# Hand-listed step order of a chunk-selecting attention and feed-forward kernel: where GpSimd issues its first loads, one copy moved to ScalarE, fewer warm-up matmuls, and two transposes moved ahead of two loads

## The chip, the cores and the metric

One Trainium2 chip, of which the program uses one core. The metric is device time in microseconds (us) of one execution; lower is better. A core has TensorE (PE: matrix products into the accumulator memory PSUM), VectorE (DVE), ScalarE (ACT), GpSimd (POOL) and SyncE (SP, which here only issues transfers). Each engine runs its own instructions in order; engines wait for each other through semaphores. Transfers (DMA) between the chip's main memory and on-chip memory are issued by SP and ACT (hardware queues, q1 and q10 in the profile) and by POOL (software queue, q0, which also converts float32 to bfloat16), and all of them are carried by the same 16 DMA engines.

## What is computed

```python
B, H, S, D = 4, 8, 768, 64;  chunk = 32;  top_k = 6
k_min, k_max = min and max of k over each chunk of 32 keys
ub = sum_d max(q * k_min, q * k_max)            # a bound for each query and chunk
top_chunks = the 6 chunks with the largest ub, among those not in the future
scores = q @ k.T / sqrt(D), masked to those chunks and to earlier positions
attn_out = softmax(scores) @ v
x = attn_out, heads side by side                 # 3072 tokens x 512
xn = x / rms(x) * rms_g
out = (silu(xn @ w_gate) * (xn @ w_val)) @ w_out # 512 -> 1536 -> 512
```

Inputs and output are float32; the products are in bfloat16, the bound `ub` in float32.

## The kernel before

The 3072 tokens are cut into 12 blocks of 256, listed in `ORDER` (L340). A block is written (b, m): batch b, third m of its sequence. The first five are (0,0), (1,0), (2,0), (3,0), (0,1); "block 0" to "block 11" count along this list. Heads are taken in two groups g = 0, 1 of four. An operation on (b, m, g) carries these numbers in its name.

What a block does in attention, with the engine and line:

- `load k…` and `load q…` (L431) fetch k and q in float32 into the tiles `kraw` and `qraw`. For blocks 0, 1 and 2 ("packed", L351) k is four transfers of 128 KB and q four more; later blocks take eight of 64 KB each. They are issued by SP, and for blocks 0 and 1 by SP and ACT in turn. `HELD` (L429) makes the first k load and the first q load of block 2 wait until the weight piece wg1 has landed, and those of block 3 until wo0 has landed.
- `load v…` (L456) fetches v in two transfers of 128 KB, e = 0 and 1, issued by POOL. `load v001` is e = 1 of block (0,0).
- `turn k`, `turn q` (DVE, L636) transpose `kraw` and `qraw` into `kT` and `qT`; `half k`, `half q` (L643 on ACT, L644 on POOL) copy them to bfloat16 (`kb`, `qb`).
- `ext0`, `ext1` (DVE, L651) take the minimum and maximum of a chunk, `dk` (POOL, L657) their difference; `bd0`, `bd1` (L676) place them in `BO`; `relu` (L731, L733) makes max(q, 0).
- `upper` (PE, L540, or L522 for m > 0) forms `ub`; `ubn`, `bar`, `top`, `mk`, `mt` (DVE, L565 to L591) choose the chunks and `swap` (L597, L601) crosses the mask to the other half of the partitions.
- `scores` (PE, L760, mask added in L771), `exp` (ACT, L810), `tri` (POOL, L780: causal triangle). For blocks 0 and 1 the scores of a block come in two parts: `a` (first 128 queries, needs no mask) and `b`.
- `values` (PE, L836), then `rden` and `norm` (DVE, L851, L855) divide and write `xnat`. `values(0,0,1)0` is group 1, first 128 tokens of block (0,0).

Then `square` (ACT, L872), `rms` (POOL, L878), `scale` (L906 on ACT, L890 on DVE). Blocks 0 to 3 go through `turn(i, …)` (PE transposes, L916) and `xsT` (L929); blocks 4 and later through `across` (L896), a transposing DMA that SP issues, two for each block (`across40` and `across41` for block 4). Blocks with m > 0 need a crossed copy of q: `qx` (L692) and, from block 4 on, four small transfers `qm0` to `qm3` on SP (L706), after which `relu` and `upper` can run.

The feed-forward (`ffn`, L937) is `wg` and `wv` (PE, L960), `tanh` (ACT, L967), `tg` (DVE, L971), `vcopy` (ACT, L979) with `hh` (POOL, L982) or `hh` on DVE (L975), then `project` (PE, L1008) and `out`. A name such as `wg(0,(0,)).4` is block 0, first 128 tokens, hidden tiles from 4 on. The weights come in thirds: wg0, wg1, wg2, wv0, wv1, wv2 (L464) and wo0 to wo2 (L469), 512 KB each in bfloat16, all issued by POOL. Hidden tiles 0 to 3 need the third 0, 4 to 7 the third 1, 8 to 11 the third 2.

Nothing decides the order at run time. `Plan.STEPS` (L47) lists all operations in one order, written as numbers: x // 8 is the operation, x % 8 its engine (0 PE, 1 ACT, 2 DVE, 3 POOL, 4 SP); each engine gets its own operations in that order. `Plan.SLOTS` (L156) gives the buffer that each operation takes. A negative number in `STEPS` is a run of warm-up matmuls (`keep_busy`, L1072) on the identity matrix, whose results nobody reads: -592 is 37 × 16 + 0, which is 18 matmuls of 512 columns into buffer F0; an even factor means 128 columns.

```python
n, slot = divmod(-x, 16)
fill[-1](n // 2, slot, n % 2)
```

Of the kernel before, what the change touches and what calls it, by code (L numbers as in the profile page):

```python
# [33 lines left out]
class Plan:  # L34
# [13 lines left out]
        27, 228, 233, 249, 244, 131, 123, 34, 155, 3, 99, 257, 276, 291, 281, 268, 299, 83, 412,  # L48
        425, 203, 67, 107, 75, 433, 420, 538, 115, 139, 315, 466, 323, 473, 482, 380, 396, 443, 490,
        545, 42, 498, 404, 307, 522, 388, 529, 506, 594, 515, 179, 611, 562, -592, -544, -320, 616,  # L50
        601, 554, 672, 626, 681, 571, 50, 457, 578, 786, 587, 634, 689, -82, -82, 792, 642, 57, 650,
        699, 848, 802, 9, 810, 857, 818, 658, 865, 826, 834, 665, 1098, 875, 841, -144, 704, 451,
        -80, 736, 912, 713, 746, 922, 754, 1107, 721, 930, 1185, -82, -114, 880, 961, 19, 1042, 731,
        889, 1114, 971, -82, 760, 897, 1058, 1049, 907, 1066, 331, 1130, 977, 1660, -211, -195,
        1248, 936, 1628, 1075, 1257, 1082, 1170, 1091, 1644, 195, -48, -128, 1192, 1684, 1177, 1362,
        1138, 1676, 1202, 1668, 1147, 1265, 1210, -48, 984, 770, 1154, 1163, 1636, 778, 1123, 946,
        1652, -49, 1368, 954, 1218, 1001, 1275, 994, 1424, 1433, 1226, -51, 1312, 1378, 8384, 1011,
        1234, 1441, 1322, 1242, 1386, 8344, 1330, 147, 1451, 1017, 1394, 1402, 339, 1280, 1410,
        8369, 1418, 1024, 1289, 1488, 347, 8336, 1498, 1297, 1034, 355, 8401, 1506, 1456, 8353,
        8480, 1307, 8410, 1537, 363, 8362, 1336, 8497, 8488, 1547, 1346, 1762, 1473, 8528, 8506,  # L60
        1465, 1851, 8513, 1354, 1483, 8536, 1778, 8545, 8379, 1553, 1706, -51, 1512, 8392, 8561,
        1522, 1530, 371, 1834, 1560, 1577, 8432, 8523, 1570, 8417, 8554, 8696, 8449, 1587, 1722,
        8688, 8458, 8721, 8571, 1593, 1730, 8584, 8705, 1802, 1739, 171, 2001, 1600, 1747, 8714,
# [1043 lines left out]
```

## Time and profile before

| what | us |
|---|---|
| three executions, median (lowest to highest) | 289.77 (289.53 to 289.91) |
| the profiled execution, whole | 291.3 |
| its span, first to last instruction | 289.5 |
| PE busy in the span | 278.6 |
| DVE busy | 215.8 |
| ACT busy | 207.0 |
| POOL busy | 167.8 |

The granted TensorE clock was 1.000 over the whole span. PE is busy for 96% of it, with 83 of its matmuls being warm-ups. The transfers move 31.94 MB, at a mean of 110 GB/s, but not evenly: the DMA engines are occupied without a break from about 2 us to 43 us, while block 0 and 1 and all weights are loaded.

How to read the rows below: in a timeline a row is start, duration, engine, line, operation, output<-input, shapes, count, and in brackets how long the engine had been idle and what the profile takes for the end of the wait. "SPq", "POOLq" or "DMA_DIRECT2D" mark the issuing of a transfer, not the transfer. The bracket names the event that came last by the profile; where the engine named had long been done, a transfer is often the true cause.

### The profile page before, as it was taken

To read this page: it belongs to the slowest core of one execution; us is meant where nothing else is said; L and a number is where in the kernel's file an instruction comes from. 1 tells how busy PE (TensorE), PEld (TensorE's weight loads), DVE (VectorE), ACT (ScalarE), POOL (GpSimd) and SP (SyncE) were. 2 spreads that over 40 slices of the span, in tenths; PEclk is the share of its full clock that TensorE was granted. 3 is DMA by queue.
4 is the path that set the end of the run, shared out by engine and by line. 5 is a ranking of instruction groups with operands and counts; after the bars stand their busy time and mean duration, and the time that the engine had idled before them with its cause. 6 is when DMAs were issued, how large, how long until landed. Compare 5 with 4: busy or idle time off the path is not lost.

```text
span 289.5 us, 11368 instructions
## 1 busy us (share of the span) xinstructions
PE 278.6 (96%) x4675; PEld 211.6 (73%) x4703; DVE 215.8 (75%) x626; ACT 207.0 (72%) x355; POOL 167.8 (58%) x268
## 2 busy tenths in 40 slices
PE   8989999999999998999999999999999999999995
PEld 2657897758877856888776786688678866588763
DVE  3978888888989999699989999987573724374341
ACT  2977887778979987867966695877679767564421
POOL 9668789979969874557693485527225206112420
PEclk9999999999999999999999999999999999999999
DMA  9999999897499494469699814913012200312023
GB/s 171 204 199 239 206 212 131 130 181 119 104 168 144 116 201 91 95 101 166 106 173 164 152 28 96 123 8 75 2 28 85 22 3 2 109 20 58 0 72 111
DMA packets 86388, 31.94 MB, mean 110 GB/s; under 512 B 74816, under 2 KB 81728, under 8 KB 86336
## 3 DMA queue, kind: packets, MB, share of 16 engines
q1 hardware_dynamic: 55616, 22.56, 33.7%
q0 software_dynamic: 29712, 7.87, 27.3%
q10 hardware_dynamic: 1008, 0.79, 1.4%
q8 instruction: 37, 0.61, 0.9%
q14 instruction: 15, 0.12, 0.1%
HBM read 28.58 MB, written 6.29 MB: 120 GB/s over the span
## 4 chain that ended last, share of the span: by engine, by line
PE 89%; DVE 3%; issue 2%; ACT 2%; SPq 1%; POOL 1%; DMA 1%; DVEq 0%; POOLq 0%
PE F L960 42%; PE F L1008 21%; PE S L760 8%; PE F L836 7%; PE F L1075 4%; PE S L771 3%; PE F L522 3%; SPq L376 1%; PE F L540 1%; ACT pt L810 1%; DVE kx L651 1%; DMA qraw<-in_q_dram 1%; PE F L916 1%; DVE kT L636 0%; DVE tg L971 0%
## 5 line engine op out<-in xcount | busy, mean ns | idle before, releaser
L810 ACT ACTIVATE pt<-S 128x1024 bf16<-128x1024 f32 (+3 forms) x104 | 85.5, 857 | 29.1 <-PE S L771 25.7
L982 POOL TENSOR_TENSOR hh<-tg,vs 128x512 bf16<-128x512 bf16 x48 | 55.1, 1157 | 43.5 <-DVE tg L971 27.8
L960 PE MATMUL F<-xsT,wg 128*128 128x256 bf16 (+1 forms) x640 | 72.2, 262 | 1.1 <-ACT pt L810 1.1
L960 PE MATMUL F<-xsT,wv 128*128 128x256 bf16 (+1 forms) x640 | 71.7, 262 | 0.1
L1008 PE MATMUL F<-wo,hh 128*128 128x512 bf16 (+1 forms) x272 | 65.6, 370 | 1.8 <-issue 0.6
L971 DVE SCALAR_TENSOR_TENSOR tg<-th,F 128x512 bf16<-128x512 bf16 x72 | 48.4, 679 | 23.9 <-ACT th L967 18.6
L960 PEld LDWEIGHTS <-wg 128*128 128x128 bf16 x640 | 55.8, 98 | 9.8 <-issue 1.5
L960 PEld LDWEIGHTS <-wv 128*128 128x128 bf16 x640 | 56.1, 98 | 7.8 <-issue 0.2
L967 ACT ACTIVATE th<-F 128x512 bf16<-128x512 f32 x72 | 42.5, 599 | 12.7 <-PE F L960 11.4
L780 POOL TENSOR_SCALAR_AFFINE_SELECT pt<-pt 128x512 bf16<-128x512 bf16 x48 | 31.9, 670 | 27.6 <-ACT pt L810 27.5
L1008 PEld LDWEIGHTS <-hh 128*128 128x128 bf16 x300 | 27.6, 98 | 25.2 <-issue 0.4
L979 ACT ACTIVATE vs<-F 128x512 bf16<-128x512 f32 x48 | 28.5, 598 | 9.8 <-PE F L960 6.6
L760 PE MATMUL S<-qb,kb 32*128 32x256 bf16 (+1 forms) x800 | 32.7, 253 | 0.9 <-ACT kb L643 0.7
L651 DVE TENSOR_REDUCE kx<-kT 128x16 f32<-128x512 f32 x48 | 31.1, 670 | 0.2
L836 PEld LDWEIGHTS <-pt 128*128 128x128 bf16 x672 | 25.5, 98 | 5.1 <-issue 1.2
L836 PE MATMUL F<-VX,pt 128*128 128x65 bf16 x672 | 27.6, 194 | 1.1 <-issue 0.7
L975 DVE TENSOR_TENSOR hh<-tg,F 128x512 bf16<-128x512 bf16 x24 | 16.1, 682 | 10.3 <-PE F L960 10.0
L760 PEld LDWEIGHTS <-kb 32*128 32x128 bf16 x800 | 13.5, 92 | 13.5 <-issue 11.6
L376 POOL DMA_DIRECT2D VX<-in_v_dram x24 | 22.9, 955 | 0.0
L636 DVE STREAM_TRANSPOSE kT<-kraw 128x512 f32<-128x512 f32 x24 | 16.4, 693 | 6.3 <-DMA kraw<-in_k_dram 4.1
L771 PE MATMUL S<-mtd,chunkrow 32*128 32x128 bf16 (+2 forms) x384 | 20.3, 203 | 0.0
L855 DVE TENSOR_TENSOR xnat<-F,rden 128x256 bf16<-128x256 f32 x48 | 19.5, 415 | 0.7
(73 smaller groups left out, 338.8 us busy)
## 6 DMA issues: line engine op xcount, KB each, us to landing
out_dram<-osb SPq DMA_DIRECT2D x23, 256.0 KB, 2.5
kraw<-in_k_dram SPq DMA_DIRECT2D x72, 64.0 KB, 3.3
qraw<-in_q_dram SPq DMA_DIRECT2D x72, 64.0 KB, 3.2
VX<-in_v_dram POOLq DMA_DIRECT2D x24, 128.0 KB, 4.8
QX<-qT SPq DMA_DIRECT2D x32, 64.0 KB, 3.0
wv<-in_moe_w_val_dram POOLq DMA_DIRECT2D x3, 512.0 KB, 11.2
wg<-in_moe_w_gate_dram POOLq DMA_DIRECT2D x3, 512.0 KB, 13.4
wo<-in_moe_w_out_dram POOLq DMA_DIRECT2D x3, 512.0 KB, 10.4
```

The source lines that it names most:

```text
L651: plan.op(f"ext{n}{J}", "DVE", 0.585, 0.67, lambda n=n, op=op: VE.tensor_reduce(out=at(kx)[:, g, n], in_=at(kT).rearrange("p h (j c x) -> ...
L760: TE.matmul(s[a // 2][:, a % 2, c0:c0 + q1 - q0], kbt[r, t, ks], qbt[r, t, q0:q1], start=(t == 0), stop=(t == 1 and not mask), skip_group_ ...
L771: TE.matmul(o, chunkrow[r, BLK * kg + P * e:BLK * kg + P * (e + 1)], mv, start=False, stop=(d == 1), skip_group_check=True)
L780: GE.affine_select(out=d, in_=d, compare_op=ALU.is_ge, fill=0.0, base=0, pattern=[[0, 4], [1, P]], channel_multiplier=-1)
L810: lambda pt=pt, hs=hs, c0=c0, c1=c1, x=sc[hp]: SE.activation(out=at(pt)[:, hs, c0:c1], in_=at(x)[:, :, c0:c1], func=ACT.Exp, scale=SCALE), ...
L836: TE.matmul(o[:, a, :], p_[:, a, off:off + P], vt[:, e, 4 * g + a, :], start=(kb_ == 0 and a == 0), stop=(kb_ == nkb - 1 and a == 3), skip ...
L960: TE.matmul(at(p_)[:, n * W:(n + 1) * W], w[:, g, ht * P:(ht + 1) * P], at(xT)[:, g, x0:x0 + W], start=(g == 0), stop=(g == NP - 1), skip_ ...
L967: plan.op(f"tanh{U}.{hp}", "ACT", 0.48, 0.6, lambda th=th, gp=gp: SE.activation(out=at(th), in_=at(gp), func=ACT.Tanh, scale=0.5), pri - 0 ...
L971: VE.scalar_tensor_tensor(out=at(tg), in0=at(th), scalar=1.0, in1=at(gp), op0=ALU.add, op1=ALU.mult), pri - 30, reads=[th, gp], writes=[tg ...
L979: plan.op(f"vcopy{U}.{hp}", "ACT", 0.48, 0.6, lambda vs=vs, vp=vp: SE.activation(out=at(vs), in_=at(vp), func=ACT.Copy), pri + 0.1, reads= ...
L982: plan.op(f"hh{U}.{hp}", "POOL", 1.11, 1.16, lambda tg=tg, vs=vs, hh=hh: GE.tensor_tensor(out=at(hh), in0=at(tg), in1=at(vs), op=ALU.mult) ...
L1008: TE.matmul(at(op)[:, cs], at(key)[:, o:o + P], wo[:, ht, cs], start=(ht == 0), stop=(ht == NHT - 1), skip_group_check=True)
```

## The change

Only `STEPS` and `SLOTS` differ. In the text of the diff nearly the whole start of `STEPS` changes:

```diff
-        27, 228, 233, 249, 244, 131, 123, 34, 155, 3, 99, 257, 276, 291, 281, 268, 299, 83, 412,
-        425, 203, 67, 107, 75, 433, 420, 538, 115, 139, 315, 466, 323, 473, 482, 380, 396, 443, 490,
-        545, 42, 498, 404, 307, 522, 388, 529, 506, 594, 515, 179, 611, 562, -592, -544, -320, 616,
...
+        27, 228, 233, 249, 244, 131, 123, 34, 155, 3, 99, 257, 276, 83, 203, 281, 67, 268, 107, 291,
+        75, 115, 412, 425, 299, 433, 420, 538, 139, 466, 380, 396, 473, 482, 490, 404, 545, 42, 498,
+        388, 522, 506, 515, 179, 594, 529, 611, 315, -288, -656, 616, 562, 601, 672, 554, 626, 571,
...
```

Written out by engine, with the names of the operations, it is this. POOL, from its sixth operation on:

```diff
 eps, BO00,
-load v000, load v001, BD02, ones9, BD00, BO01, BD01, BO02, ones1,
-wv0, wg1, load v100, wg0,
-bd1(0,0,0), ones6, relu(0,0,0), dk(0,0,1), bd1(0,0,1), tri(0,0,0)a, tri(0,0,1)a,
-load v101, half q(1,0,0), half, tri(0,0,0)b, rms(0,(0,)), tri(0,0,1)b, wv1,
-dk(1,0,0), bd1(1,0,0), ones8, dk(1,0,1), bd1(1,0,1), half k(1,0,1), tri(1,0,0)a, rms(0,(1,)),
+BD02, ones9, BD00, BO01, load v000, BD01, BO02, load v001, ones1,
+bd1(0,0,0), ones6, relu(0,0,0), wv0, dk(0,0,1), bd1(0,0,1), wg1, tri(0,0,0)a, load v100,
+tri(0,0,1)a, half q(1,0,0), wg0, half, tri(0,0,0)b, rms(0,(0,)), dk(1,0,0), bd1(1,0,0),
+tri(0,0,1)b, load v101, ones8, dk(1,0,1), bd1(1,0,1), tri(1,0,0)a, wv1, rms(0,(1,)),
 ones2, tri(1,0,1)a, wg2, wv2, wo0, tri(1,0,0)b, wo1,
...
```

ACT, DVE and SP:

```diff
 ACT: half q(1,0,1), exp(1,0,0)0a1,
+half k(1,0,1),
 square01, exp(1,0,1)0a0,
...
 DVE: bd0(1,0,0), turn q(1,0,1),
-relu(1,0,1), ext1(1,0,1), ubn(1,0,0), bar(1,0,0), rden(0,0,0)1, bd0(1,0,1), norm(0,0,0)1,
+ext1(1,0,1), rden(0,0,0)1, norm(0,0,0)1, ubn(1,0,0), relu(1,0,1), bar(1,0,0), bd0(1,0,1),
 rden(0,0,1)1, norm(0,0,1)1, top(1,0,0), xsT(0,(0,)),
...
 SP: load k1210, store2.1,
+across40, across41,
 load q1210, load q1220,
-across40, across41,
 load q1201, qm0(2,1),
...
```

PE, up to the last warm-up (W18 is 18 warm-ups of 512 columns, w17 is 17 of 128 columns):

```diff
-W18, w17, w10, upper(0,0,0), scores(0,0,0)0a, W2, W2, upper(0,0,1), scores(0,0,1)0a, W4,
-scores(0,0,0)0b, W2, values(0,0,0)0, values(0,0,1)0, W2, W3, scores(0,0,1)0b, W2, values(0,0,0)1,
-W6, w6, scores(1,0,0)0a, values(0,0,1)1, W1, w4, upper(1,0,0), W1, turn(0,(0,)), W1, upper(1,0,1),
-scores(1,0,1)0a, W1, values(1,0,0)0,
+w9, W20, upper(0,0,0), scores(0,0,0)0a, W5, upper(0,0,1), scores(0,0,1)0a, W6,
+scores(0,0,0)0b, W1, values(0,0,0)0, values(0,0,1)0, W4, scores(0,0,1)0b, W4, values(0,0,0)1,
+W4, scores(1,0,0)0a, upper(1,0,0), values(0,0,1)1, W2, turn(0,(0,)), W1, upper(1,0,1),
+scores(1,0,1)0a, values(1,0,0)0,
 wg(0,(0,)).4, wv(0,(0,)).0, scores(1,0,0)0b, turn(0,(1,)), values(1,0,1)0, wg(0,(0,)).0,
 scores(1,0,1)0b, wg(0,(1,)).0, values(1,0,0)1, wv(0,(1,)).0, wg(0,(1,)).4, wv(0,(1,)).4,
-W1,
 values(1,0,1)1,
...
```

That is 46 wide and 37 narrow warm-ups before, 47 wide and 9 narrow ones after. From there on every engine has the same operations in the same order as before, but for SP's two transposes; in `SLOTS` about 160 PE operations along the whole kernel take another of the four PSUM buffers F0 to F3.

272 rows, old and new, of tables (SLOTS, STEPS) are left out of this document.

## The prediction

> **What bounds the kernel now.** First the busy times by stage. The columns after a stretch are its length, the busy times of PE, PE's weight loads, DVE, ACT and POOL, then the clock, the DMA share and GB/s.
>
> ```profile
> 45.00:100.00 55.00, 54.45 (x902) 41.12 (x911) 49.12 (x157) 45.94 (x85) 47.46 (x72) 1.00 0.87 141
> ```
>
> From 45 us on PE is busy for 54.45 of 55 us, and its order there does not change. Time can go only in the start and in the few holes later. The start looks as full, but warm-ups fill it, so PE's share says nothing there. The chain of waits (start, length, what) shows what the start hangs on:
>
> ```profile
> 17.43 1.30 DVE kT L636 x2
> ...
> 24.72 1.79 PE F L960 x32
> ```
>
> The first feed-forward products stand at its end, DVE's `turn k` of block (1,0) near its head. The timeline of DVE, and of PE in its last row:
>
> ```profile
> 14.87 0.74 DVE L855 TENSOR_TENSOR xnat<-F,rden 128x256 bf16<-128x256 f32 x2
> 17.43 1.30 DVE L636 STREAM_TRANSPOSE kT<-kraw 128x512 f32<-128x512 f32 x2 [1.82 <-ACT pt L810]
> 20.51 0.70 DVE L636 STREAM_TRANSPOSE qT<-qraw 128x512 f32<-128x512 f32 x1
> 23.63 0.67 DVE L929 TENSOR_TENSOR xsT<-F,rmsg 128x512 bf16<-128x512 bf16 x1
> 24.56 1.05 PE L960 MATMUL F<-xsT,wg 128*128 128x128 bf16 x16
> ```
>
> DVE stands idle for 1.82 us before `turn k`. The row names ACT's `pt`, which `turn k` does not read; it reads `kraw`. The four k loads of block (1,0), first and last issue and landing times:
>
> ```profile
> L376 SPq DMA_DIRECT2D kraw<-in_k_dram x4: 311/368/511, 6.4 to 8.2; - x4
> DMA to landing us min/median/max: 7.4/8.3/9.1
> ```
>
> The last, issued at 8.2, lands 9.1 later, at 17.3, and DVE starts at 17.43. So this landing, and not DVE's or PE's work, sets the time of the first feed-forward product. What shares the DMA engines with it was issued by POOL, and the rates by stage show at what cost:
>
> ```profile
> 1.97 1.99 POOL L376 DMA_DIRECT2D VX<-in_v_dram  x2
> 5.32 0.77 POOL L376 DMA_DIRECT2D wv<-in_moe_w_val_dram  x1
> 6.00:12.00 6.00, 6.00 (x111) 3.86 (x109) 5.85 (x19) 5.95 (x8) 4.23 (x10) 1.00 1.59 165
> 12.00:15.50 3.50, 3.48 (x68) 1.77 (x60) 2.77 (x14) 3.20 (x11) 2.53 (x4) 1.00 1.18 259
> 29.50:40.00 10.50, 9.85 (x186) 9.42 (x186) 9.41 (x18) 8.81 (x19) 7.85 (x16) 1.00 1.24 206
> ```
>
> While v is moving, all queues together reach 165 GB/s; with weights beside k and q 259; weights alone 206, so that a third of 512 KB takes 2.5 us.
>
> **Part by part: the loads.** Four memsets now stand before `load v000` and two more before `load v001`: v starts 0.8 to 1.3 us later. wv0 moves behind `relu(0,0,0)`, from 5.3 to 9.2; wg1 behind `bd1(0,0,1)`, which ends at 11.3 in the row below; v100 behind the first `tri`, to 12.6; wg0 behind `half q(1,0,0)`, to 15.2. q of block 0 then shares with less, which lets k of block (1,0) be issued sooner, and no weight can flow before about 12. From 12.0 to 17.3 k still had to move most of its 4 × 128 KB; at 259 GB/s that is 2.0 us, so the landing is estimated at 14.0. Bounds: 12.5, if q lands first and v gets out of the way, and 17.3, if v alone was the brake.
>
> DVE must then first finish `norm(0,0,1)0`, for which POOL's second `tri` and PE's `values` are needed:
>
> ```profile
> 10.97 0.31 POOL L676 TENSOR_TENSOR BO<-kx,own 128x32 f32<-128x32 f32 x1
> 13.10 0.63 POOL L780 TENSOR_SCALAR_AFFINE_SELECT pt<-pt 128x512 bf16<-128x512 bf16 x1 [0.96 <-ACT pt L810]
> 14.31 0.42 PE L836 MATMUL F<-VX,pt 128*128 128x65 bf16 x8
> ```
>
> wg1's issue (0.8 us, as wv's above) now stands ahead of the first `tri`, v100's (1.0, half of the pair's 1.99) ahead of the second. This is a wait that the change adds: 11.2 + 0.8 + 0.65 + 0.95 puts the second `tri` at 13.55 in place of 13.10, and it ends at 14.15; behind it POOL's `half q(1,0,0)` and `rms` are 0.5 and 0.3 late, but ACT's `scale` needs that `rms` only after `half k(1,0,0)`. PE reaches `values` at 14.1, with one warm-up less ahead of it, does both groups by 14.4, and the norms end at 15.45 (14.87 + 0.74 = 15.61 before). DVE can take `turn k` there: 17.43 - 15.45 = 2.0 us gained, if k has landed by 15.25. The estimate leaves 1.2 us to spare.
>
> From there the chain keeps its length. `relu(1,0,1)` now follows `ext1`, `rden`, `norm` and `ubn`, but these stood between it and `xsT` anyway; `xsT` ends 7.0 us after `turn k` starts (23.63 + 0.67 - 17.43 = 6.9 before), at 22.45, and PE has `upper(1,0,1)`, `scores` and `values` done by 22.3. `wg` starts at 22.5 in place of 24.56: **-2.0**. Bounds: -2.4, if `tri` isn't late, and 0, with k at 17.3.
>
> **half k(1,0,1) on ACT** costs what a copy of this size takes there:
>
> ```profile
> 21.24 1.07 ACT L643 ACTIVATE qb<-qT 128x512 bf16<-128x512 f32 x1 [1.10 <-DVE qT L636]
> 23.66 0.63 ACT L872 ACTIVATE junk<-xnat 128x512 bf16<-128x512 bf16 x1 [1.08 <-DVE xnat L855]
> ```
>
> ACT's idle 1.08 before `square01` hides the 1.07; without that cover `square01`, `exp(1,0,1)a` and all behind them on ACT would be 1.1 late. POOL gets to `tri(1,0,0)a` sooner, which nothing waits for long. I take 0.
>
> **Warm-ups.** Before, they run until `upper(0,0,0)` starts, though its `relu` on POOL was done at 9.21 (8.80 + 0.41). Now they are 9 narrow and 20 wide ones. Below, the whole run, and the wide ones before and after 6.9 us:
>
> ```profile
> 1.42 8.29 PE L1075 MATMUL F<-ident 128*128 128x512 bf16 x45 [1.42 <-POOL ident masks.py:199]
> 8.80 0.41 POOL L733 TENSOR_SCALAR qraw<-qT 128x128 f32<-128x128 f32 x1
> L1075 PE MATMUL F<-ident 128*128 128x512 bf16 x13 | 5.7, 631 | 1.4 <-POOL ident masks.py:199 1.4
> L1075 PE MATMUL F<-ident 128*128 128x512 bf16 x6 | 1.7, 422 | 0.0
> ```
>
> 13 take 5.7 us (0.44 each) while PE is slow; the next, at most 0.28 each, are quick. So 1.0 for the narrow ones (a quarter as wide), 11 × 0.44 and 9 × 0.28: they end at 9.8 at the latest, 0.1 after the old run's end. The later runs stop about where the next product is ready. Off the chain, 0, between -0.3 and +0.1. The Trainium skill, TensorE: Matmul & The Clock Gate (Part 1, What's actually happening), says that the window which opens the clock runs freely, so that the slow phase can end earlier or later in another execution; no run so far shows two.
>
> Most of PE's operations take another PSUM buffer; each is a bank that some reader must leave first. With the order unchanged I take 0; a bad pick would show as a short PE wait.
>
> **The transposes.** SP, then the landing of the two transposes, PE, POOL, PE:
>
> ```profile
> 107.02 0.96 SPq L376 DMA_DIRECT2D qraw<-in_q_dram  x2
> 108.08 3.30 SPq L896 DMA_TRANSPOSE xsT<-xs  x2
> DMA to landing us min/median/max: 2.5/2.9/3.4
> 112.76 1.03 PE L960 MATMUL F<-xsT,wg 128*128 128x256 bf16 x8 [1.05 <-ACT pt L810]
> 118.69 1.20 POOL L733 TENSOR_SCALAR qraw<-QX 128x512 f32<-128x512 f32 x2 [6.45 <-DMA QX<-qT]
> 119.10 0.95 SPq L376 DMA_DIRECT2D qraw<-in_q_dram  x2
> 119.86 0.45 PE L522 MATMUL F<-QX,BD 64*32 64x128 f32 x16
> ```
>
> PE idles 1.05 us for block 4's `xsT`: the second transpose, issued near 110.1, lands 2.5 later, at 112.6. Without the two loads ahead (0.96) it lands at 111.65 and the idle all but goes. But `upper(2,1)` starts at 119.86, just as its `relu` ends (118.69 + 1.20), and that `relu` waited for the `qm` transfers, which SP issues behind the same two loads and two transposes as before. So 0.95 reappears there as a new wait. The loads go 3.3 later; the last pieces of their block go out at 119.1 anyway. I take -0.1; ends -1.05 (the `qm` come sooner by as much) and +0.3 (they come later).
>
> **Does it last?** SP resumes block 3's loads when wo0 lands, and then issues almost without pause:
>
> ```profile
> 23.16 16.52 SPq L376 DMA_DIRECT2D kraw<-in_k_dram  x6
> SPq L376 <- DMA wo<-in_moe_w_out_dram: 12.0, 1, 12.0
> 61.90 1.42 SPq L376 DMA_DIRECT2D kraw<-in_k_dram  x3
> 65.85 0.76 SPq L706 DMA_DIRECT2D QX<-qT  x1
> ```
>
> From 63.3 to 65.85 it waits for POOL's `qx`. So SP, even if wo0 lands no earlier, has 2.5 us in hand and can follow a chain that is 2.0 ahead; the rest comes in the same order.
>
> **Sum.** -2.0 and -0.1 on the profiled span of 289.5 make 287.4. That execution took 291.3 in all; the median of three, 289.77, lies 0.27 above the span. 289.77 - 2.1 = **287.7**.
>
> **Rivals.** *Weights late (slower).* wg0's transfer, and its first use:
>
> ```profile
> L376 POOL DMA_DIRECT2D wg<-in_moe_w_gate_dram x1: 802/802/802, 7.7 to 7.7; - x1
> DMA to landing us min/median/max: 15.2/15.2/15.2
> 27.23 1.05 PE L960 MATMUL F<-xsT,wg 128*128 128x128 bf16 x16
> ```
>
> Issued at 15.2 with the same 15.2, it lands at 30.4, and PE gets at 30.6 what it had at 27.23: +3.4, 293.1. It slows the kernel once wg0 lands after 27.2. For it: block 2's loads, free once wg1 lands, now meet it. Against: most of the 15.2 was queueing behind v0, wv0, wg1 and v100; now wv0, wg1 and wg0 itself at 2.5 us each and v100, flowing from 12 on beside k, put it at 21 to 23.5, against a need at 25.2 (27.23 - 2.0). 0.17.
>
> *Gain partly lost.* k lands at 16 to 17, or block 4's loads come no earlier and hold DVE after 60. Half of it: 1 us, 288.8. 0.17.
>
> *The moved issues don't free k.* The v packets, only shifted, were the brake, and k lands at 17.3 again. The 165 GB/s speaks for it; against it, that after 12 k ran beside weights alone. 289.7. 0.11.
>
> *PE's clock opens late.* 20 wide ones at 0.44 run to 11.2, so that block 0 is 1.5 late and most of the gain goes: 289.2. The rule above allows it, the one trace does not show it. 0.04.
>
> **How the numbers follow.** The forecast has the remaining 0.51, with 287.2 to 288.3 as its own range. About 0.2% (0.58 us) is what a measurement of this kernel can tell from no change. Faster: 0.51 + 0.17 = 0.68. Same: 0.11 + 0.04 = 0.15. Slower: 0.17. The range leaves out most of the late weights, above 290.3, and, below 286.7, the ends -2.4 and -1.05 coming together.
>
> **What would show it.** Right: the last k of (1,0) landing before 15.3; `turn k` on DVE at 15.5 straight behind the norms; the first `wg` near 22.5; wg0 landed before 25; no new PE idle from 22 to 45; at block 4 the 1.05 gone and a wait of nearly that size before `upper(2,1)`. Wrong: `turn k` after 17, PE idle before `wg` or `wv` in the twenties, ACT late at `square01`, or PE's first `upper` after 10.

## The result, and the profile after

The changed kernel is slower, by 0.6 to 0.8%. Its median over 11 executions is 292.36 us (291.28 to 294.22) against 289.91 us (288.92 to 291.40, also 11) for the kernel before; the ratio is 1.0077 with a 95% interval of 1.0051 to 1.0102. A second measurement gave 1.0060 (1.0033 to 1.0087). Ratios here and below leave out executions that were disturbed; medians in the table take in all. Forecast was 287.7 us, faster.

The profiled execution took 291.38 us (span 289.6), hardly more than the 291.3 us of the one profiled before. So these two traces cannot show the whole difference. They still show most of the mechanism. First the timeline of the changed kernel, VectorE's rows and then TensorE's (start, duration, engine, line, operation, tiles, count, in brackets the idle time before):

```profile
14.71 0.74 DVE L855 TENSOR_TENSOR xnat<-F,rden 128x256 bf16<-128x256 f32 x2
15.37 1.29 DVE L636 STREAM_TRANSPOSE kT<-kraw 128x512 f32<-128x512 f32 x2
21.42 0.67 DVE L929 TENSOR_TENSOR xsT<-F,rmsg 128x512 bf16<-128x512 bf16 x1
...
22.23 1.05 PE L960 MATMUL F<-xsT,wg 128*128 128x128 bf16 x16
...
24.90 1.05 PE L960 MATMUL F<-xsT,wg 128*128 128x128 bf16 x16
...
28.36 0.39 PE L960 MATMUL F<-xsT,wg 128*128 128x128 bf16 x4
30.26 0.83 PE L960 MATMUL F<-xsT,wg 128*128 128x128 bf16 x12 [1.51 <-issue]
30.93 1.06 PE L960 MATMUL F<-xsT,wv 128*128 128x128 bf16 x16
...
109.37 1.05 PE L836 MATMUL F<-VX,pt 128*128 128x65 bf16 x28
110.27 1.03 PE L960 MATMUL F<-xsT,wg 128*128 128x256 bf16 x8
```

The start is as forecast: `turn k` follows the norms at once, and the first `wg` starts at 22.23 instead of 24.56. The 1.05 us ahead of block 4's `wg` are gone as well (last two rows). New in its size is the stop of 1.51 us at 30.3; the kernel before has a shorter one near that time, ahead of another operation:

```profile
30.46 0.33 PE L836 MATMUL F<-VX,pt 128*128 128x65 bf16 x5 [0.65 <-issue]
```

The other new ones come between 125 and 129 us:

```profile
125.39 1.03 PE L960 MATMUL F<-xsT,wg 128*128 128x256 bf16 x8 [0.56 <-DVE tg L971]
127.17 0.80 PE L836 MATMUL F<-VX,pt 128*128 128x65 bf16 x20 [0.75 <-DVE tg L971]
128.36 0.92 PE L836 MATMUL F<-VX,pt 128*128 128x65 bf16 x24 [0.40 <-DVE hh L975]
```

Twenty traces were taken in all. To compare nineteen of them (the one with block 2 held back, below, is left out), take TensorE's product instructions one by one and subtract their start in a reference trace: the second trace of the kernel before (289.73 us in all, near its median). The medians of this difference at six places, in us, negative where TensorE is ahead, are worked out from the traces:

| trace | 26 | 38 | 100 | 116 | 136 | 275 | whole time |
|---|---|---|---|---|---|---|---|
| before, first trace | 0.90 | 0.95 | 1.01 | 1.44 | 1.62 | 1.62 | 291.3 |
| before, mean of 7 traces with the old start | 0.83 | 0.83 | 0.85 | 0.45 | 0.51 | 0.52 | 290.2 |
| after | -1.43 | -0.67 | -0.13 | -0.96 | 1.16 | 1.76 | 291.4 |
| after, second trace | -1.26 | -0.39 | -0.35 | -0.20 | 1.30 | 1.94 | 291.6 |
| new start and swap, mean of 8 traces | -1.35 | -0.24 | 0.13 | -0.45 | 1.06 | 1.37 | 291.0 |
| new start, swap, `qm` in a row, mean of 3 | -1.11 | -0.01 | 0.36 | -0.43 | -0.43 | 0.09 | 289.8 |

Read along the rows: the new start is 2.1 us ahead at 26 us (0.83 to -1.28, the mean of all 12 traces that have it), 1.0 us at 38 us and 0.7 us at 100 us. Between 116 and 136 us the kernels with new start and swap lose 1.5 us on average (0.4 to 2.1 in single traces), those with the old start or with `qm` in a row nothing on average.

### The profile page after: what moved, and what is told of

It reads as the page before. It is cut to its first block, busy times and chain, and to the rows that moved or that the text cites. A ratio compares the mean times of both kernels' runs of the same rounds, so it can differ in the third digit from the quotient of the medians.

```text
span 289.6 us, 11341 instructions
## 1 busy us (share of the span) xinstructions
PE 279.9 (97%) x4676; PEld 210.3 (73%) x4676; DVE 216.5 (75%) x626; ACT 207.6 (72%) x356; POOL 166.9 (58%) x267
## 3 DMA queue, kind: packets, MB, share of 16 engines
q1 hardware_dynamic: 55616, 22.56, 34.6%
q0 software_dynamic: 29712, 7.87, 27.3%
## 4 chain that ended last, share of the span: by engine, by line
PE 79%; DVE 7%; DMA 5%; issue 2%; POOL 2%; ACT 2%; SPq 2%; ACTq 0%; DVEq 0%; POOLq 0%
PE F L960 39%; PE F L1008 19%; PE S L760 7%; PE F L836 7%; PE S L771 3%; DMA kraw<-in_k_dram 3%; PE F L522 2%; DMA xsT<-xs 1%; PE F L1075 1%; PE F L540 1%; DVE xnat L855 1%; SPq L376 1%; DVE tg L971 1%; DVE kx L651 1%; DVE kT L636 1%
## 5 line engine op out<-in xcount | busy, mean ns | idle before, releaser
L982 POOL TENSOR_TENSOR hh<-tg,vs 128x512 bf16<-128x512 bf16 x48 | 55.8, 1172 | 43.9 <-DVE tg L971 28.3
L1008 PE MATMUL F<-wo,hh 128*128 128x512 bf16 (+1 forms) x300 | 68.8, 371 | 0.1
L780 POOL TENSOR_SCALAR_AFFINE_SELECT pt<-pt 128x512 bf16<-128x512 bf16 x48 | 31.3, 658 | 26.0 <-ACT pt L810 25.9
```

Source lines behind the costliest of these rows:

```text
L780: GE.affine_select(out=d, in_=d, compare_op=ALU.is_ge, fill=0.0, base=0, pattern=[[0, 4], [1, P]], channel_multiplier=-1)
L982: plan.op(f"hh{U}.{hp}", "POOL", 1.11, 1.16, lambda tg=tg, vs=vs, hh=hh: GE.tensor_tensor(out=at(hh), in0=at(tg), in1=at(vs), op=ALU.mult) ...
L1008: TE.matmul(at(op)[:, cs], at(key)[:, o:o + P], wo[:, ht, cs], start=(ht == 0), stop=(ht == NHT - 1), skip_group_check=True)
```

## The experiments

All kernels beside the kernel before on the same chip; n counts executions.

| kernel | median us (n) | before us | ratio, 95% interval |
|---|---|---|---|
| before again | 290.11 (12) | 290.01 | 1.0010, 0.9978 to 1.0043 |
| after again | 291.79 (12) | 290.01 | 1.0060, 1.0033 to 1.0087 |
| swap only | 290.26 (12) | 290.01 | 0.9996, 0.9963 to 1.0029 |
| new start only | 291.82 (12) | 290.01 | 1.0024, 0.9990 to 1.0059 |
| after, tg first | 291.68 (8) | 290.31 | 1.0056, 1.0025 to 1.0087 |
| after, qm in a row | 290.88 (9) | 290.31 | 1.0029, 0.9990 to 1.0068 |
| before, swap, qm in a row | 289.19 (10) | 290.31 | 0.9969, 0.9955 to 0.9983 |
| the same again | 289.94 (12) | 290.06 | 0.9985, 0.9957 to 1.0012 |
| after, more warm-ups | 291.26 (12) | 289.81 | 1.0038, 1.0009 to 1.0066 |
| after, fewer warm-ups | 292.09 (10) | 289.81 | 1.0067, 1.0041 to 1.0093 |
| before, fewer warm-ups | 289.79 (10) | 289.81 | 1.0008, 0.9990 to 1.0026 |
| after, qm in a row, more warm-ups | 290.60 (12) | 289.81 | 1.0014, 0.9989 to 1.0039 |
| after, block 3 held until wv2 | 291.49 (12) | 290.39 | 1.0021, 0.9984 to 1.0057 |
| before, swap, qm in a row, wv2 | 289.85 (12) | 290.39 | 0.9981, 0.9961 to 1.0002 |
| after, qm in a row, more warm-ups, wv2 | 289.81 (12) | 290.39 | 0.9984, 0.9958 to 1.0010 |
| after, wv1 early | 291.05 (12) | 290.39 | 1.0016, 0.9982 to 1.0050 |
| after, rms first | 291.39 (12) | 290.06 | 1.0038, 1.0008 to 1.0068 |

### Both kernels again

> The kernel before, unchanged, as a kernel of its own. Every theory expects a ratio of 1.000 within 0.003; the run is for the spread and for a second trace of it. The theory that the changed kernel gives its gain back at three places (block 0's weights, 125 to 128 us, 162 us) expects this trace to have the same gaps on TensorE as the first one of it: about 1.05 us at 112.8 us, at most 0.4 us between 123 and 130 us, first wg at 24.6 us, and a whole time near 291.3 us. The rival, that the first trace of it was an unusually long execution, expects a whole time near 289.9 us and a gap that is smaller here by over 0.5 us, most likely the one at 112.8 us.

> The changed kernel, unchanged, as a kernel of its own. Every theory expects a ratio of 1.005 to 1.010 (291.4 to 292.8 us). If what gives the gain back is set by the program, this trace has the gaps of the first one again: about 1.5 us at 30.3 us, 1.7 us in all between 125 and 129 us, 0.3 us at 162 us. If it is set by how transfers happened to fall, the gaps stand elsewhere or differ by over 0.5 us.

The kernel before ran true to itself (1.001), and the rival about its first trace is right: the second one took 289.73 us. Its first `wg` starts earlier, and its gap at 112 us is not there (0.51 us at 110.0 and 0.28 us at 113.1 stand in its place):

```profile
23.66 1.05 PE L960 MATMUL F<-xsT,wg 128*128 128x128 bf16 x16
```

So of the 24.56 on which the forecast was built, 0.9 us belonged to that one execution, and the stop of 1.05 us was not a fixed property either. In the changed kernel the program sets the stops: the second trace has 1.64 us at 30.6 and 1.30 us in all between 125 and 129 again. But its swap brings little: TensorE has a stop of 0.99 us at 110.1, ahead of `values`.

### Each half of the change alone

```diff
 before, SP: load k1210, store2.1,
+across40, across41,
 load q1210, load q1220,
-across40, across41,
```

> The kernel before with one thing of the change: SP issues block 4's two transposes ahead of the loads q1210 and q1220. Theory A (the swap removes the 1.05 us gap at 112.8 us but block 4's next step is set by SP's qm transfers and VectorE, which don't move): the gap at 112.8 us goes, and by 130 us TensorE has given 0.8 us or more of it back; 289.5 to 290.3 us. Theory B (the swap pays in full): 288.8 to 289.1 us. Theory C (the two later loads cost more than the transposes gain): 290.5 us or more.

The new start only is the changed kernel with these four in their old order.

> The changed kernel with SP's old order back: q1210 and q1220 ahead of the transposes. Theory A (the start pays 2.3 us at 25 us and 1.1 to 1.4 us by 110 us; what is lost is lost after 112 us, whatever the order there): TensorE is 1.1 us ahead of before until 110 us, the gap at 112 us is back with 0.3 to 1.0 us, and the time is within 0.8 us of the changed kernel's. Theory B (the swap is what makes the kernel slower): 288.0 to 289.0 us. Theory C (the start itself is what makes it slower, in most executions): 291.5 us or more, and TensorE not ahead by 110 us.

The swap alone is level with before (0.9996). In its trace the gap at 112 us is gone and TensorE gets 1.0 us ahead from 100 to 116 us and keeps it to the end, as theory B has it, in an execution of 288.77 us; the median does not follow, and 0.3% either way stays open. The start alone is not faster either (1.0024, interval up to 1.0059): 1.25 us ahead at 26 us, 0.42 at 38, nothing at 100. Neither half is slower by itself beyond doubt; the two together are. Of the theories for the start alone none came true as a whole: TensorE's lead is gone by 110 us, against A, and the ratio leaves open whether the start makes the kernel slower, as C has it.

### The stop at 30 us: wv1 or TensorE's own instructions

```diff
-HELD = {2:("wg",1),3:("wo",0)}
+HELD = {2:("wv",1),3:("wo",0)}
```

> The changed kernel, but block 2's q and k loads are held until wv1 has landed instead of wg1. For the gap of 1.4 to 1.6 us at 30.3 us, which the profile calls issue. Theory A (TensorE stands for wv1, which lands at 30.9 us since the weights share the transfer engines with block 2's loads): wv1 lands 1.5 us or more earlier, and the gap shrinks by as much. Theory B (an issue gap of TensorE itself, as fetching of its instructions): the gap stays over 1 us although wv1 has landed. Block 2 is late for both, by 3 us or more, and the whole time says nothing.

The issue of wv1 and the time to its landing, in the changed kernel and then with block 2 held back:

```profile
L376 POOL DMA_DIRECT2D wv<-in_moe_w_val_dram x1: 821/821/821, 21.3 to 21.3; - x1
DMA to landing us min/median/max: 9.5/9.5/9.5
```

```profile
L376 POOL DMA_DIRECT2D wv<-in_moe_w_val_dram x1: 821/821/821, 21.2 to 21.2; - x1
DMA to landing us min/median/max: 6.1/6.1/6.1
```

With block 2's loads out of the way, wv1 lands at 27.3 instead of 30.8, and the timeline of TensorE runs through the place of the stop:

```profile
28.29 1.06 PE L960 MATMUL F<-xsT,wg 128*128 128x128 bf16 x16
```

The stop is gone and wv1 lands 3.5 us earlier, as theory A has it. But this run moved two things at once, and the traces speak for theory B, that TensorE's instructions come late. The profile lists transfers of a kind of its own, here over the whole execution of the changed kernel (number, MB, share of the engines' time):

```profile
q8 instruction: 36, 0.59, 0.9%
```

They are 16 KB each and ride on the same transfer engines. The times of the one in question, of the stop and of wv1, worked out from the traces, in us:

| trace | q8 transfer | product after the stop | stop | wv1 lands | first needed |
|---|---|---|---|---|---|
| before | 27.74 to 29.10 | 30.46 | 0.65 | 29.2 | 32.36 |
| before, second trace | 26.69 to 28.00 | 29.50 | 0.61 | 29.0 | 31.41 |
| after | 27.95 to 29.00 | 30.26 | 1.51 | 30.8 | 30.89 |
| after, second trace | 28.00 to 29.08 | 30.55 | 1.64 | 31.2 | 31.21 |
| after, fewer warm-ups | 28.35 to 29.43 | 30.81 | 1.07 | 31.6 | 31.62 |
| after, more warm-ups | 27.20 to 28.14 | 29.71 | 1.36 | 31.0 | 31.05 |
| after, wv1 early | 27.73 to 28.79 | 30.21 | 1.42 | 30.5 | 30.83 |
| after, block 2 held back | 26.18 to 27.12 | 28.51 | none | 27.3 | 29.12 |

"First needed" is the first weight load of the `wv` that reads wv1. Three things tell the two theories apart. First, the stop ends before wv1 lands, by 0.3 to 1.3 us in the five traces with the new start that have it here, so wv1 can't be what ends it. Second, its place is counted in instructions and not in operations: in all twelve traces with the new start and block 2 not held back it stands ahead of TensorE's 477th matmul, warm-ups included, which is after 4, 10 and 0 matmuls of the same `wg` with 20, 14 and 24 wide warm-ups; with the old start it is the 478th, in the five of seven traces that have a stop. Third, that matmul starts 1.26 to 1.65 us after the end of the q8 transfer in all twenty traces, also in the three where TensorE does not stand; that q8 carries TensorE's instructions is inferred from this.

So TensorE stands for its next instructions. On average their transfer ends at 28.9 us with the old start and at 28.95 with the new: it did not get faster when TensorE did, and the stop grew from 0.6 to 1.5 us on average. What sets the time of this transfer is open; with block 2's loads out of the way it ended at 27.12. Had the instructions been there, wv1 would have held TensorE almost as long: in the changed kernel's traces `wv` starts within 0.1 us of its landing, and in the one with more warm-ups the profile itself shows 0.46 us of waiting for it. In the run with block 2 held back, block 2 came 9.7 us late, as said; the whole time (301.02 us) means nothing. The counterpart moves only the issue of wv1:

```diff
 after, POOL: load v101,
+wv1,
 ones8, dk(1,0,1), bd1(1,0,1), tri(1,0,0)a,
-wv1,
 rms(0,(1,))
```

> The changed kernel with wv1 issued right behind load v101, ahead of GpSimd's ones8, dk(1,0,1), bd1(1,0,1) and tri(1,0,0)a: about 20.0 us instead of 21.3 us. Theory A (issue time sets it: queued ahead of block 2's last k loads it lands 1 us or more earlier): wv1 lands by 29.8 us, the gap at 30.3 us is 0.5 us or less, TensorE is 0.8 us further ahead at 36 us. Theory B (bytes set it: what wv1 gains block 2's k loads or wg2 lose): wv1 lands earlier, but TensorE's place at 36 us changes by under 0.4 us, and the time is that of the changed kernel, 291.4 to 292.3 us.

Theory B holds in the trace. Issued 1.3 us earlier, wv1 takes 1.0 us longer:

```profile
L376 POOL DMA_DIRECT2D wv<-in_moe_w_val_dram x1: 759/759/759, 20.0 to 20.0; - x1
DMA to landing us min/median/max: 10.5/10.5/10.5
```

It lands at 30.5 instead of 30.8, the stop is 1.42 us, and TensorE is 0.80 us ahead at 36 us against 0.67 in the changed kernel. Two limits hold it there. The instruction transfer ends at 28.79 (29.00 in the changed kernel), so that `wv` starts 0.33 us after wv1 is there. And up to about 43 us the transfer engines have no break: wv1's landing moves by 0.3 us where its issue moves by 1.3. What it queues behind fits that: in the changed kernel the k loads of block 2 are all out by 23.1 us instead of 25.6 (24.7 in the second trace of before), and wv1, issued at 21.3 instead of 18.0, lands 1.6 us later. The median was nearer to before (1.0016) than Theory B allows; its interval overlaps that of the changed kernel.

### The stops at 125 us: first tries

```diff
 after, DVE: scale50, scale51,
+tg(4,(0,1)).8,
 qx(1,2,0),
-tg(4,(0,1)).8,
```

> The changed kernel, but on VectorE tg(4,(0,1)).8 runs ahead of qx(1,2,0). In both traces of the changed kernel tg starts at 124.7 to 124.8 us, behind two scale operations of 1.11 us and a qx of 1.4 to 1.6 us that overlap GpSimd's hh, and TensorE then stands still for 1.3 to 1.7 us between 125 and 129 us. Theory A (that pile-up on VectorE gives back what the swap gained): the gaps there fall under 0.6 us and the time to 290.2 to 291.0 us. Theory B (the median is lost elsewhere, for example by run-to-run stalls that these traces don't show): the gaps fall, the median stays at 291.5 us or more. Theory C (the pile-up is only moved: the scales still end late and their transposes with them): the gaps fall and come back by 165 us.

```diff
 after, SP: qm0(2,1),
-load q3100, load q3130,
 qm3(2,1), qm1(2,1), qm2(2,1),
+load q3100, load q3130,
```

> The changed kernel, but SP issues qm0, qm3, qm1, qm2 of (2,1) in a row, ahead of the loads q3100 and q3130. Theory A (GpSimd's relu(2,1) waits for qm at 117.2 to 117.5 us, so that GpSimd's later hh falls on VectorE's scale and qx): relu starts by 116.4 us, scale is 0.8 us earlier, and the gaps between 125 and 129 us fall by 0.6 us or more; 290.4 to 291.2 us. Theory B (GpSimd's relu doesn't matter): no change, 291.5 to 292.3 us. Theory C (the loads are then too late for turn q(3,1,0)): VectorE waits for q at 125 us and the time is 292 us or more.

> The kernel before with the swap and with qm0, qm3, qm1, qm2 of (2,1) in a row. Theory A (swap and earlier qm pay together, since the 1.05 us at 112 us goes and GpSimd isn't late): 288.6 to 289.3 us, faster than before by 0.7 us or more. Theory B (as the swap alone measured, nothing is left of it): 289.7 to 290.5 us.

> The kernel before with the swap and qm in a row, a second time, to see whether it is faster than before for good. If the first result (ratio 0.997) holds: 0.995 to 0.999. If it was chance: 0.999 to 1.002.

With `tg` first the stops were 0.89 and 0.40 us, TensorE still lost 1.7 us from 116 to 136 us, and the time stayed (1.0056): it only moved one operation within the pile-up. With `qm` in a row these stops are gone (0.12 us are left), and so is the loss from 116 to 136 us, in all six traces of kernels that have it, on both starts. In time it took off 0.3 to 0.5% (1.0029 against 1.0060 and 1.0077, the intervals overlap). Theory A of that run had the scale 0.8 us earlier; it came 0.13 us earlier. On the old start, swap and `qm` in a row are faster than before: 0.9969, then 0.9985 with an interval that reaches 1.0012.

Why it works is seen on GpSimd and VectorE. First the changed kernel, GpSimd's timeline from `relu(2,1)` on and VectorE's from `scale50` on:

```profile
117.16 1.20 POOL L733 TENSOR_SCALAR qraw<-QX 128x512 f32<-128x512 f32 x2 [6.54 <-DMA qraw<-in_q_dram]
...
120.31 0.70 POOL L880 TENSOR_TENSOR ri_all<-ri_all,mhalf 128x2 f32<-128x2 f32 x1
120.98 0.64 POOL L780 TENSOR_SCALAR_AFFINE_SELECT pt<-pt 128x512 bf16<-128x512 bf16 x1
121.86 0.80 POOL L780 TENSOR_SCALAR_AFFINE_SELECT pt<-pt 128x512 bf16<-128x512 bf16 x1 [0.24 <-ACT pt L810]
122.63 1.58 POOL L982 TENSOR_TENSOR hh<-tg,vs 128x512 bf16<-128x512 bf16 x1
...
121.05 2.15 DVE L890 SCALAR_TENSOR_TENSOR xs<-xnat,ri_all,gB 128x512 bf16<-128x512 bf16 x2 [0.74 <-POOL ri_all L880]
123.12 1.62 DVE L692 COPY QX<-qT 128x512 f32<-128x512 f32 x1
124.66 0.67 DVE L971 SCALAR_TENSOR_TENSOR tg<-th,F 128x512 bf16<-128x512 bf16 x1
```

The same with `qm` in a row:

```profile
115.94 1.20 POOL L733 TENSOR_SCALAR qraw<-QX 128x512 f32<-128x512 f32 x2 [4.85 <-DMA QX<-qT]
...
119.67 0.71 POOL L880 TENSOR_TENSOR ri_all<-ri_all,mhalf 128x2 f32<-128x2 f32 x1
121.06 1.11 POOL L780 TENSOR_SCALAR_AFFINE_SELECT pt<-pt 128x512 bf16<-128x512 bf16 x1 [0.68 <-ACT pt L810]
122.51 0.69 POOL L780 TENSOR_SCALAR_AFFINE_SELECT pt<-pt 128x512 bf16<-128x512 bf16 x1 [0.34 <-ACT pt L810]
123.18 1.32 POOL L982 TENSOR_TENSOR hh<-tg,vs 128x512 bf16<-128x512 bf16 x1
...
120.92 1.79 DVE L890 SCALAR_TENSOR_TENSOR xs<-xnat,ri_all,gB 128x512 bf16<-128x512 bf16 x2
122.64 0.85 DVE L692 COPY QX<-qT 128x512 f32<-128x512 f32 x1
123.41 0.67 DVE L971 SCALAR_TENSOR_TENSOR tg<-th,F 128x512 bf16<-128x512 bf16 x1
...
128.85 0.41 DVE L692 COPY QX<-qT 128x512 f32<-128x512 f32 x1
```

`scale50` waits for `rms` (L880) on GpSimd. In the changed kernel GpSimd is late, its first `tri` finds its `exp` ready and starts 0.07 us ahead of `scale50`. Then each scale takes 1.11 us, `hh` starts 0.49 us ahead of `qx`, `qx` takes 1.62 us where it takes 0.41 us undisturbed (last row), and `tg`, for which TensorE waits, comes 3.61 us after the first scale. With `qm` in a row GpSimd is early enough to wait for that `exp`: `scale50` is first by 0.14 us and takes 0.75 us, `tri` takes 1.11 us instead of 0.64, the second scale still takes 1.13, but `qx` starts 0.54 us ahead of `hh` and takes 0.85 us, and `tg` comes after 2.49 us.

Here VectorE and GpSimd slow each other from operation to operation. The Trainium skill, SBUF — State Buffer (Terms), says that the two arbitrate for one pair of ports, which is locked for a whole instruction, so that the loser waits. The trace agrees in kind: of the first pair, whoever is second has 1.11 us in place of 0.64 or 0.75. In size the wait is shorter: an estimate by that rule, the second starting afresh at the end of the first, gives 1.32 us for the scale and 1.25 for `tri`.

Which pair matters is seen over all twenty traces. In seven of them, all with new start and swap, `hh` starts ahead of `qx`; `qx` then takes 1.03 to 1.62 us, and TensorE's stops there add up to 1.28 to 1.71 us. In the other thirteen `qx` is first and takes 0.85 us, and the stops add up to 0.1 to 0.5 us. The first pair does not decide: with the new start alone, and in the changed kernel with 24 warm-ups, `tri` is ahead of `scale50` by 0.07 us too, yet `qx` is ahead of `hh` and the stops are 0.39 and 0.40 us.

### Is SP's late start behind it?

```diff
-HELD = {2:("wg",1),3:("wo",0)}
+HELD = {2:("wg",1),3:("wv",2)}
```

> The changed kernel, but block 3's first k and q loads are held until wv2 has landed (36 us) instead of wo0 (38.5 us). Theory A (SP, which is issuing almost without pause from there to 120 us, starts too late for a TensorE that runs ahead, and its lateness ends as the pile-up at 121 to 128 us): SP waits for qx at 65 us by 2 us or more again, the gaps between 124 and 129 us fall from 1.4 to 1.9 us to under 0.6 us, and the time is 290.2 to 291.0 us. Theory B (SP's start doesn't matter, the pile-up has its cause at 112 us itself): the gaps stay, 291.4 to 292.3 us. Theory C (the earlier loads delay wo0 to wo2 and cost as much as they bring): a new gap of TensorE between 40 and 60 us.

> The kernel before with the swap, qm in a row, and block 3's loads held until wv2 instead of wo0. On the old start SP had 2.5 us in hand at 65 us. Theory A: no more than 0.4 us better than without it (289.2 us): 288.8 to 289.3 us. Theory B (SP's start matters for this start too): 288.5 us or less.

> The changed kernel with qm in a row, 24 wide warm-ups and block 3's loads held until wv2. Theory A (with SP no longer late, the new start keeps what it has at 36 us, some 0.5 us): 288.7 to 289.6 us. Theory B (something of the new start is lost in a place not yet found): 290.0 us or more.

In the changed kernel SP starts block 3's loads at 38.5 and has 0.52 us in hand at 64.5, where it had 2.52:

```profile
62.52 1.43 SPq L376 DMA_DIRECT2D kraw<-in_k_dram  x3
64.47 0.76 SPq L706 DMA_DIRECT2D QX<-qT  x1
```

Held only until wv2, SP starts at 36.0 and has 1.37 us there, but the stops at 124 to 128 us add up to 1.63 us as before: theory A falls. What carries the delay is nearer, the two loads between `qm0` and the other `qm` (2.37 us, then 1.87 us for three `qm`):

```profile
110.80 2.37 SPq L376 DMA_DIRECT2D qraw<-in_q_dram  x2
113.22 1.87 SPq L706 DMA_DIRECT2D QX<-qT  x3
```

The time came down in part (1.0021, up to 1.0057, from 8 executions), which the trace does not explain. On the old start the hold brings nothing to be seen (0.9981 against 0.9969 and 0.9985), which neither theory of that run had. The third kernel, with `qm` in a row, more warm-ups and the hold on the new start, is at 0.9984, between its two theories and level with `qm` in a row and the hold on the old start (0.9981): with these three mends the loss is gone, and the new start neither gains nor loses by what the runs can tell.

### The warm-ups

The first warm-ups of the changed kernel, in its two traces:

```profile
1.42 7.53 PE L1075 MATMUL F<-ident 128*128 128x128 bf16 x29 [1.42 <-POOL ident masks.py:199]
```

```profile
1.42 6.46 PE L1075 MATMUL F<-ident 128*128 128x128 bf16 x29 [1.42 <-POOL ident masks.py:199]
8.97 0.44 PE L540 MATMUL F<-qT,BO 64*64 64x32 f32 x16 [1.08 <-DVE BO L676]
```

The same 29 matmuls end at 8.95 or at 7.88, where TensorE then stands for 1.08 us. Three traces with the old start (swap only, and twice swap with `qm` in a row) had 1.25 to 1.52 us there and a clock cut to a half shortly after; the first of them by stretches (length, busy times of PE, PE's weight loads, DVE, ACT, POOL, then clock, DMA share, GB/s):

```profile
8.00:10.00 2.00, 0.75 (x24) 0.54 (x20) 1.20 (x3) 0.86 (x2) 1.26 (x4) 1.00 1.59 185
10.00:12.00 2.00, 1.91 (x35) 1.05 (x28) 2.00 (x8) 2.00 (x4) 0.51 (x3) 0.78 1.20 194
12.00:14.00 2.00, 2.00 (x43) 1.14 (x42) 1.16 (x7) 0.98 (x3) 0.70 (x2) 0.50 1.16 278
```

So the number of wide warm-ups at the start was varied: 24 and 14 instead of 20 in the changed kernel, 12 instead of 18 in the one before.

> The changed kernel with 24 wide warm-ups ahead of upper(0,0,0) instead of 20, about 0.9 us more. So far the mean granted clock was under 0.996 in about a third of the executions of kernels with the new start, at a time 1.5 to 2.5 us above their others, and in about a quarter with the old start, at 0.4 us above. In every trace with such a dip of an undisturbed head TensorE stood 1.25 us or more ahead of upper(0,0,0) (between 8 and 10 us); with 1.08 us or less there was none. Theory A (the shorter warm-up cover leaves TensorE idle there, and the clock that is then withdrawn costs the new start 2 us in a third of the executions): under one in ten executions below 0.996, median 290.9 to 291.5 us. Theory B (the dips come from elsewhere): as many as before, 291.5 to 292.4 us.

> The changed kernel with 14 wide warm-ups there instead of 20, so that TensorE stands still for 1.6 to 2.5 us ahead of upper(0,0,0). Theory A (idle time there takes the clock, and the new start has no slack for it): the clock falls below 0.996 in nearly every execution, to about 0.5 between 11 and 16 us in the trace, and the time is 1.0 to 2.5 us above the changed kernel's, 293 to 294.5 us. Theory B (the clock has no part): 291.5 to 292.4 us.

> The kernel before with 12 wide warm-ups at the very start instead of 18. Theory A (the old start is bound by the k transfer of block (1,0), which lands at 16 to 17 us, so that a clock withdrawn at 11 to 16 us is mostly hidden): below 0.996 in nearly every execution, and 290.2 to 290.9 us, 0.2 to 0.7 us above before. Theory B (a withdrawn clock costs both starts the same): 291.5 us or more. Theory C (idle time there doesn't take the clock): at 0.998 or above in most executions.

> The changed kernel with qm0, qm3, qm1, qm2 of (2,1) in a row and with 24 wide warm-ups. Theory A (the pile-up at 121 to 128 us and the clock together are what made the change slower): 289.5 to 290.4 us, level with before or better. Theory B (the new start loses as such, through wv1 at 30 us): 290.5 us or more, against 289.2 us for the kernel before with swap and qm in a row.

The theories that hang on the stop ahead of `upper` fall. With 14 the stop is 2.42 us, yet the clock stays at 1.00 in the profiled execution; it was low in 5 of 10, at a median like the changed kernel's:

```profile
9.46 0.44 PE L540 MATMUL F<-qT,BO 64*64 64x32 f32 x16 [2.42 <-DVE BO L676]
...
12.00:14.00 2.00, 2.00 (x46) 1.11 (x46) 1.78 (x14) 1.86 (x6) 1.99 (x3) 1.00 1.13 208
```

On the old start fewer warm-ups cost nothing (1.0008), and the clock was low in 4 of 10, not in nearly all. With 24 the median is 291.26 (1.0038), some 0.3% better than 1.0060 and 1.0077 with overlapping intervals; the clock was low in 2 of 12. Fewer dips are not all of that: of the executions in the ratio, those with a mean clock of 0.996 or more have a median of 290.99 us, against 291.62 and 291.73 in the two measurements of the changed kernel. With `qm` in a row besides, the time is 290.60 us (1.0014), between the two theories of that run. The trace with 24 shows the dip elsewhere, behind the stop at 28.3 us (stretches of 1 us, then TensorE's rows):

```profile
29.00:30.00 1.00, 0.29 (x6) 0.29 (x6) 0.00 (x0) 0.30 (x1) 0.00 (x0) 1.00 1.24 228
...
31.00:32.00 1.00, 0.58 (x6) 0.68 (x7) 0.84 (x3) 1.00 (x2) 1.00 (x3) 0.71 1.27 208
32.00:33.00 1.00, 1.00 (x13) 1.00 (x11) 1.00 (x2) 0.01 (x1) 1.00 (x2) 0.50 1.22 209
...
29.71 1.05 PE L960 MATMUL F<-xsT,wg 128*128 128x128 bf16 x16 [1.36 <-issue]
31.42 1.86 PE L960 MATMUL F<-xsT,wv 128*128 128x128 bf16 x16 [0.66 <-DVE tg L971]
```

From 31.4 to 34.6 the clock is near 0.5, and the `wv` of 1.06 us takes 1.86. This trace goes from 1.6 us ahead at 28 us to 1.3 behind at 38; the stop, with wv1 behind it, and the dip are both in that. The dips of the old start fell at 11 to 16 us: swap only is 1.7 us late at 14 us and 0.8 at 28, the two with `qm` in a row are 1.7 and 1.8 us late at 26 us, so the wait for k does not always hide them. Over all kernels the mean clock was under 0.996 in 31% of the 81 executions counted in the ratios with the new start and 20 warm-ups, in 21% of 34 with 24, and in 19% of 201 with the old start, and these took about 1.5 us more on the new start and 0.8 on the old. Counted out, 0.31 × 1.5 - 0.19 × 0.8 is 0.3 us: an estimate of what the dips cost the change. That the new start's come behind the stop at 30 us is seen in one trace only; six other traces with a stop of 1.5 to 2.0 us there have no dip behind it.

### Is the order the cause?

```diff
 after, POOL: half k(2,1,1),
-half q(1,2,0), rms(5,(0,1)),
+rms(5,(0,1)), half q(1,2,0),
```

> The changed kernel, but GpSimd does rms(5,(0,1)) ahead of half q(1,2,0), so that VectorE's scale50 can start about 0.6 us earlier, while GpSimd copies, instead of together with its tri. Theory A (who comes first to the SBUF port that the two engines share decides: with tri first, two scales and qx are each held up by GpSimd): scale50 starts ahead of tri, the gaps of TensorE between 121 and 130 us fall from 1.3 to 1.7 us to 0.5 us or less, and the time to 290.0 to 291.2 us. Theory B (the order only goes along with something else, such as a late relu): scale50 starts earlier and the gaps stay over 1 us; 291.4 to 292.3 us.

The stops fall to 0.40 us, as theory A has it, but not for its reason. GpSimd's copy, not its `tri`, now stands beside `scale50`, and it is first by 0.08 us, so that `scale50` still takes 1.07 us. What changed is further on: `qx` starts 0.54 us ahead of `hh` and takes 0.85 us, and `tg` comes 2.81 us after the first scale (3.61 before). The time does not follow (291.39, 1.0038): in this trace the swap brings nothing (a stop of 0.88 us at 110.7), TensorE is 1.33 us back between 28 and 32 us, and it is again 1.18 us late at 136. So two edits that put `qx` ahead of `hh` take the stops down, and all twenty traces fit that order; each edit also moved other work on GpSimd. That these stops alone make the kernel slower is not shown.

## Why the prediction was wrong

*The transfers and `turn k`: right.* The k loads of block (1,0) and their landing:

```profile
L376 SPq DMA_DIRECT2D kraw<-in_k_dram x4: 312/368/427, 6.2 to 7.9; - x4
DMA to landing us min/median/max: 6.0/6.3/6.4
```

The last lands at 14.1 (forecast 14.0), DVE's `turn k` starts at 15.37 (15.45), the first `wg` at 22.23 (22.5). But the size was read off one execution: against the second trace of before the gain is 1.43 us, not 2.33.

*"Does it last?": the step that failed first.* The forecast kept the whole 2.0 us to the end; at 100 us the traces with the new start have 0.7 of it on average. The step looked at SP's queue and at wg0. wg0 lands at 23.0, as worked out, and is used at 24.90. Two other transfers of the stretch without a break were not asked for, and the list of signs promised no new idle time from 22 to 45 us. TensorE's own next instructions arrive at 28.9 us with either start: the kernel before stood 0.6 us for them on average, the changed one, being ahead, 1.5 us. And wv1, which had landed 3.2 us before its use in the first trace of before (29.2 against 32.36), lands 1.6 us later and is used as it lands. On average 1.1 of 2.1 us are lost between 26 and 38 us; the longer stop is 0.9 of that. Why the instruction transfer comes when it does stays open.

*SP's hand of 2.5 us: right in kind.* wo0 landed 0.6 us later, SP had 0.5 us left and kept up. It is not where the time went.

*The transposes: a wrong size and a wrong place.* Forecast was that the 1.05 us vanish and 0.95 come back before `upper(2,1)`, since `qm` stay where they are, -0.1 in all. The first half was right; with the swap TensorE gains 0.6 to 0.8 us on average from 100 to 116 us. `upper(2,1)` has no stop. What the `qm` held up was GpSimd's `relu`, behind it `rms`, and through the order of `hh` and `qx` it costs 1.5 us on average from 116 to 136 us. The term was -0.1, with +0.3 as its upper end; together with the new start it measures about +0.9 us in the traces. The rival with the right sign was priced at 293.1 for a late wg0, not for this.

*half k on ACT: taken as 0, and 0 as far as the traces show.* ACT's `square01` follows it at 21.45 without idle time, and VectorE's `xsT` isn't late for it.

*The warm-ups: sized on the slow case.* The run of 29 was to end at 9.8 at the latest, "0, between -0.3 and +0.1". It ended at 7.9 to 9.0 in the traces of such kernels, and a stop behind it was not in the list. The rule cited there, that the window which opens the clock runs freely (the Trainium skill, TensorE: Matmul & The Clock Gate, Part 1, What's actually happening), agrees with the 6.46 and 7.53 us for the same work. The stop itself costs nothing that the runs show.

*The PSUM slots: 0 from 45 to 105 us,* where the changed kernel has no stop over 0.14 us. At 125.39 a `wg` waits for the slot that a late `tg` still reads; there the pile-up is late, not the slot.

*The base.* The median was compared with a span: whole time and span differ by 1.7 to 1.9 us in most executions. This did not touch the difference forecast, but it hid that the profiled execution (291.3 in all) was 1.4 us longer than the median.

What stays open: the medians of the two kernels differ by 1.8 to 2.45 us; their traces by 1.3 (1.85 for the two of the changed kernel at 275 us, 0.58 for three with the old start and no swap). Of the rest the dips are an estimated 0.3 us. Single stops of 0.3 to 0.9 us at 72, 76, 86, 162 and 190 us stand in one or two traces with the new start each; no run ties them to a part of the change.

## What to carry to other kernels

Where the transfer engines have no break, an engine that gets ahead meets transfers that did not move with it: list every load in that stretch with its first use, and TensorE's instruction transfers too. Before a stop is put down to a transfer, compare its end with the landing, and count at which instruction it stands in several variants: an experiment that removes the stop can move two causes at once. Before sizing a gain on one profiled execution, compare its whole time with the median, and take a second trace: here 0.9 of 2.3 us and the stop to be mended were that execution's own. An engine that falls 0.5 us behind another can change who is first at a resource that they share, and the cost then depends on that order, not on the 0.5 us.

## What was not expected of the hardware

- Two operations that VectorE and GpSimd start 0.07 to 0.14 us apart cost the second 0.4 to 0.5 us. `qx` took 0.41 us undisturbed, 0.85 us where it started ahead of GpSimd's `hh`, and up to 1.62 us where it started behind it.
- TensorE stood for its own instructions: in all twenty traces its 477th or 478th matmul starts 1.26 to 1.65 us after a 16 KB instruction transfer ends. The stop is shown as "issue", and four warm-ups more or six fewer move it by as many matmuls.
- The granted clock fell to 0.50 after a stop of 1.25 us at 9 us, and did not after one of 2.42 us at the same place.
